# Scan operands and anchors in PSUM, the state's sum on VectorE, no idle products in the loop

## The chip, the core and the metric

The kernel runs on one core of one Trainium2 chip. The metric is the device time of one execution in microseconds. The engines run at the same time, each through its own list of instructions in order, and wait for each other by semaphores: TensorE (PE in the profile; its weight loads are PEld), VectorE (DVE), ScalarE (ACT), GpSimd (POOL) and SyncE (SP), which here only issues DMAs. SBUF is the large on-chip memory; PSUM is the small one of eight banks that TensorE writes its products to and that VectorE and ScalarE, but not GpSimd, use as well in this kernel.

## What is computed

A linear attention with decay, then a mixture of eight experts with one expert a token, then a gated feed-forward layer. The change lies in the first part and in the gate behind it:

```python
# r, k, v, w: (2, 8, 768, 48); u: (8, 48)
for t in range(768):
    cur = einsum('bhd,bhe->bhde', u * k_t, v_t)
    y[:, :, t] = einsum('bhd,bhde->bhe', r_t, state + cur)
    state = w_t[:, :, :, None] * state + einsum('bhd,bhe->bhde', k_t, v_t)
x = y as (1536, 384)
logits = x @ w_gate                    # (1536, 8); the first of the largest is the expert
disp[e, pos] = x of the tokens of e    # in order of the tokens
h = maximum(disp @ w1[e], 0); out = gate weight * (h @ w2[e])
out = (silu(out @ w_gate2) * (out @ w_val)) @ w_out
```

## The kernel before

**Chunks.** The 1536 tokens are cut into twelve chunks `u` of 128 (`C`), six for each batch (`UPB`); a chunk is two halves of 64 (`HC`). The heads lie as four pairs (`NP`), two heads of 48 in the 128 partitions. Within a chunk the recurrence is written as products: VectorE makes running products of the decays, `scores(u)` makes a masked matrix of scores, `values(u)` multiplies it with the values and adds what the state of the earlier chunks gives, and `state(u)` makes the next state.

**VectorE's preparation of a chunk.** `prep1(u)`: two scans X (L369), one for each half, over 264 columns: a running product of the decays, begun anew at each head pair by a constant second operand, `xinit`, in SBUF. `anchored(u)`: a reciprocal (L377) of every eighth column of X, written to every eighth column of `anch[u % 2]`, which is zero elsewhere. `prep2(u)`: two scans R (L415) over 256 columns, which multiply with the decays `wm` (copied by ScalarE in `prep0`) and add the anchors; then two products M (L421, L424) of k and r with X and R, which `scores(u)` and the later products read; then `prep3`, the product rk (L434).

**The other VectorE work of the loop.** `xrow(u)`: x (L533), the output y from PSUM plus the chunk's own term aV (GpSimd, L449). In `state(u)`: d (L516), the decay over the chunk's border, and the new state Sc (L519), which is the PSUM tile psP times d. `expand(u)` (ScalarE) puts the state into the tile Sb for `values(u+1)`. Small steps of the gate's choice are put between these by `tick()` when a group of four chunks is complete.

**TensorE's order in iteration u** (u = 0 to 9): `state(u)`: for chunks with an earlier state first a product of the identity with Sc (L509), which begins the sum in psP, then sixteen small products (L513); `warm`: products of constants into a bank that nobody reads (L458), three an iteration from u = 2 on; `scores(u+1)` (L469), whose results ScalarE copies out (L471) and GpSimd masks with two selects (L472); transposes of k (L480); products for the own term and the gate's logits (L441, L559) and transposes of x (L547) in `gate_t(u-1)`; `values(u)` (L494, L499); `columns` (L576), the last product for the logits. VectorE prepares chunk u+2 in iteration u, so TensorE's scores of chunk u+1 need the M that VectorE made in the iteration before. No state is made for chunks 5 and 11. `check(u)` lets ScalarE read X and anch (L386) to add up a measure of range. GpSimd has two selects and one aV an iteration, later also the scatters.

The order on every engine is that of the program; the schedule is written by hand, and the framework adds the semaphores. For PSUM it keeps any two accesses of different engines to the same bank of one tile in the order of the program, two reads included. The loop is

```python
    for u in range(NU - 2):
        if u:
            prep0(u + 2); prep1(u + 2)
        xrow(u - 1); state(u); anchored(u + 2)
        warm((7, 4)[u] if u < 2 else 3, ps1, "xT")
        scores(u + 1)
        if u: own(u)
        kgtok(u + 1); gate_t(u - 1, ...)
        expand(u); load_dm(u + 4); zero(NZ)
        ...                                  # count and place a complete group
        prep2(u + 2); check(u + 2)
        values(u); columns(u - 1, ...)
```

and chunk 10 and 11 are finished by a written-out tail (L948 on), with one state (chunk 10) and VectorE's own aV. Behind it come the experts (L1297, L1315) and the feed-forward layer (L1418, L1441).

Of the kernel before, what the change touches and what calls it, by code (L numbers as in the profile page):

```python
# [24 lines left out]
C = 128  # L25
# [4 lines left out]
G = 8  # L30
# [12 lines left out]
def build(tc, cap, dm, tk, vt, ub, cst, wg, w1, w2, wgate, wval, wout, out):  # L43
# [239 lines left out]
    ac = at.enter_context(tc.tile_pool(name="ac", bufs=1))  # L283
    xinit = ac.tile([128, 2, NP, XW], F32, name="xinit")
    csb = ac.tile([128, 3 * E], F32, name="csb")
# [4 lines left out]
    tri = ac.tile([128, 128], BF16, name="tri")  # L290
    ones = ac.tile([128, 128], BF16, name="ones")
    slots = ac.tile([128, NU], I32, name="slots")
# [7 lines left out]
    dmt = [ep.tile([128, DMW], F32, name=f"dm{i}", bufs=1) for i in range(3)]  # L300
    anch = [ep.tile([128, 2 * (NP * HC + G - 1)], F32, name=f"anch{i}", bufs=1) for i in range(2)]
    wm = [ep.tile([128, 2, NP, HC], F32, name=f"wm{i}", bufs=1) for i in range(2)]
# [4 lines left out]
    ps1 = at.enter_context(tc.tile_pool(name="ps1", bufs=1, space=PSUM))  # L307
    psY = at.enter_context(tc.tile_pool(name="psY", bufs=2, space=PSUM))

    vts, Xf, Xt, Mt, kgt, Sc, At, yt, xt, xgt, xgs, av, rkt, a8s, lgt = ({} for _ in range(15))  # L310
# [5 lines left out]

    def anchors(x, h, o):

        return x[:, h, :, h * o:h * o + HC - G + 1:G]

# [39 lines left out]
    def prep1(u):  # L360


        if u >= NU:
            return
        W = dmt[u % 3][:, 0:2 * NP * XW].rearrange("p (h a j) -> p h a j", h=2, a=NP)
        Xf[u] = ap3.tile([128, 2 * (NP * XW + G + 1)], F32, tag="X", name="X")
        X = Xt[u] = halved(Xf[u], XW)
        for h in range(2):
            nc.vector.tensor_tensor_scan(out=run(X[:, h], h), data0=run(W[:, h], h), data1=run(xinit[:, h], h),  # L369
                                         initial=0.0, op0=ALU.mult, op1=ALU.max)  # L370
            tick()

    def anchored(u):

        if u >= NU:
            return
        nc.vector.reciprocal(out=each8(anch[u % 2], HC), in_=each8(Xf[u], XW))  # L377
        tick()

    def check(u):  # L380

        if u >= NU:
            return
        for i, t in enumerate((each8(Xf[u], XW), each8(anch[u % 2], HC))):
            j = gp.tile([128, 2, NP, HC // G], F32, tag="sum", name="sum")
            nc.scalar.activation(out=j, in_=t, func=AF.Copy, accum_out=total[:, 2 * u + i:2 * u + i + 1])  # L386
# [22 lines left out]
    def prep2(u):  # L409
# [4 lines left out]
        for h in range(2):  # L414
            nc.vector.tensor_tensor_scan(out=run(Rt[:, h], 1 - h), data0=run(wm[u % 2][:, h], 1 - h),  # L415
                                         data1=run(halved(anch[u % 2], HC)[:, h], 1 - h),
                                         initial=0.0, op0=ALU.mult, op1=ALU.add)
            tick()
# [34 lines left out]
    def warm(n, ps=None, tag="T"):  # L453

        ps = (ps or psA).tile([128, 512], F32, tag=tag if ps else "A0", name="psW")
        x = xinit.rearrange("p h a j -> p (h a j)").bitcast(BF16)[:, 0:512]
        for _ in range(n):
            nc.tensor.matmul(ps, ones, x, start=True, stop=True)  # L458

# [24 lines left out]
    def values(u, ps=range(NP)):  # L484

        if not ps[0]:
            yt[u] = psY.tile([128, DM], F32, tag="y", name="y")
        y, A = yt[u], At[u]
        V = vts[u]
# [12 lines left out]
    def state(u):  # L502

        if not (u + 1) % UPB:
            return
        P = ps1.tile([128, NP, D], F32, tag="P", name="psP")
        k = kgt.pop(u)
        if u % UPB:
            nc.tensor.matmul(P, ident, Sc[u], start=True, stop=False, skip_group_check=True)  # L509
        for p in range(NP):  # L510
            for g in range(2):
                c0 = D * (2 * p + g)
                nc.tensor.matmul(P[64 * g:64 * g + 64, p, :], k[:, p, 64 * g:64 * g + 64], vts[u][:, c0:c0 + D],  # L513
                                 start=not u % UPB, stop=True, skip_group_check=True)
        d = ap2.tile([128, NP], F32, tag="d", name="d")
        nc.vector.tensor_tensor(out=d, in0=Xt[u][:, 1, :, XW - 1], in1=Xt[u + 1][:, 0, :, 0], op=ALU.mult)  # L516
        tick()
        s = Sc[u + 1] = ap2.tile([128, NP, D], F32, tag="Sc", name="Sc")
        nc.vector.tensor_tensor(out=s, in0=P, in1=d.unsqueeze(2).to_broadcast([128, NP, D]), op=ALU.mult)  # L519
        tick()  # L520
# [8 lines left out]
    def xrow(u):  # L529
        if u < 0:  # L530
            return
        x = xt[u] = gp.tile([128, DM], F32, tag="x", name="x", bufs=7)
        nc.vector.tensor_tensor(out=x, in0=yt.pop(u), in1=av.pop(u), op=ALU.add)  # L533
        tick()
# [27 lines left out]
    def logits_to(u):  # L562
        g = group[u]
        if g not in lgt:
            lgt[g] = ps1.tile([128, len(g), 3 * E], F32, tag="P" if g[-1] == NU - 3 else "lg", name="lg")
        return lgt[g][:, u - g[0]]
# [6 lines left out]
    def columns(u, w, q):  # L573

        to = logits_to(w)
        nc.tensor.matmul(to[:, 0:2 * E], gss.pop(u), fold[:, 0:2 * E], start=True, stop=True)  # L576
        a8s[q] = gp.tile([128, H], F32, tag="a8", name="a8")
        nc.scalar.copy(out=a8s[q], in_=to[:, E:2 * E])
# [22 lines left out]
    def choose(us, weigh=weigh):  # L601

        n = len(us)
        u0, u1 = us[0], us[-1] + 1
        lg = lgt[us][:, :, 0:E]

# [40 lines left out]
    def count(us):  # L647

        u0, n = us[0] // 4 * 4, len(us)
        pc = lgt[us][:, :, 2 * E:]  # L650
        adds = [(ohacc, us[0])] * (u0 > 0) + [(ohs[:, q, :], max(us[0], q + 1)) for q in range(u0, us[-1])]
# [204 lines left out]
    nc.vector.memset(xinit, TINY)  # L856
    nc.vector.memset(xinit[:, 0, :, HC:HC + 1], 1.0)
    nc.vector.memset(xinit[:, 1, :, 1:2], 1.0)
    for i in range(2):
        nc.gpsimd.memset(wm[i], 0.0)  # L860
        nc.vector.memset(anch[i], 0.0)
    nc.vector.memset(ones, 1.0)
    prep0(0)
# [16 lines left out]
    anchored(1)  # L880
    prep2(1)
    prep0(2)
    prep1(2)
    for i in range(2):
# [3 lines left out]
    for u in range(NU - 2):  # L888
        chosen, counted = ended.get(u - 2), ended.get(u - 3)
        if u:  # L890
            prep0(u + 2)
            prep1(u + 2)
        xrow(u - 1)
        state(u)
        anchored(u + 2)
        warm((7, 4)[u] if u < 2 else 3, ps1, "xT")
        scores(u + 1)
# [5 lines left out]
        else:  # L903
# [5 lines left out]
            gss.update((q, gs[:, C * q:C * q + C]) for q in range(2))  # L909
            warm(2, ps1, "lg")  # L910
        expand(u)
# [7 lines left out]
        if not u:  # L919
            check(1)  # L920
            nc.vector.tensor_copy(out=tri, in_=before)
        check(u + 2)
        if u:
            values(u)
            columns(u - 1, max(u - 2, 0), u + 1)
        else:
            values(u)
            for q in range(2):
                to = logits_to(q)
                nc.tensor.matmul(to[:, 0:E], gss.pop(q), fold[:, E:2 * E], start=True, stop=True)  # L930
            a8 = gp.tile([128, 2, H], F32, tag="a82", name="a82")
            nc.scalar.copy(out=a8, in_=lgt[group[0]][:, 0:2, 0:E])
            for q in range(2):
# [27 lines left out]
    for f in c4:  # L961
        f()
    state(u)
    values(u, [0])
    warm(1, ps1, "xT")
# [595 lines left out]
```

## Time and profile before

| | us |
|---|---|
| median of 3 runs (465.39 to 465.67) | 465.55 |
| the profiled execution | 465.57 |
| its span, first to last instruction | 463.9 |
| TensorE busy in the span | 450.2 (97%) |
| VectorE busy | 331.0 (71%) |
| ScalarE busy | 238.8 (51%) |
| GpSimd busy | 70.9 (15%) |

The busy shares are means over stages with different bounds: TensorE's 97% over the span doesn't say what bounds the attention loop, which lies between about 14 and 79 us. A stage is read from its own windows and its own timeline. In a timeline the first number is the start, the second what the instruction took to its last write, and the next independent instruction of VectorE may start some 0.1 us before that end; "x2" is two like instructions in a row, taken together. What stands in brackets behind a row is the idle time before it and what ended it. The spans on GpSimd are rough, and a few records of matmuls are missing (two of three products at 32.36, for one).

### The profile page before, as it was taken

What the parts mean: (1) busy time and instruction counts of PE and PEld (TensorE: products, weight loads), DVE (VectorE), ACT (ScalarE), POOL (GpSimd) and SP (SyncE); (2) the same over time, 40 slices, a digit from 0 to 9 for tenths busy, and PEclk for the clock granted to TensorE, in tenths of its full rate; (3) what the DMA queues carried; (4) which work ended last, traced back from release to release, by engine and by line L of the source; (5) the groups of instructions that cost most, each with busy time, mean ns of one, the idle gap of its engine ahead of it and who ended that gap; (6) DMA issues with size and microseconds to landing.
All of it is one profiled execution on the core that took longest, in us unless ns stands there. A gap on an engine that the chain in (4) does not pass through costs nothing.

```text
span 463.9 us, 9305 instructions
## 1 busy us (share of the span) xinstructions
PE 450.2 (97%) x3565; PEld 397.8 (86%) x3576; DVE 331.0 (71%) x690; ACT 238.8 (51%) x561; POOL 70.9 (15%) x94
## 2 busy tenths in 40 slices
PE   7998999999999999999999999999999999999994
PEld 3676767889999999999988888888888888888884
DVE  8999999877887945858599876665678585434241
ACT  4556685666877866674446454544443352231120
POOL 3324355540000000000000650000000000003033
PEclk9999999999999999999999999999999999999999
DMA  7798994139999944336134455222200000001011
GB/s 247 219 290 266 314 279 163 70 103 305 378 350 361 357 171 144 91 116 199 42 101 131 75 68 70 68 68 69 68 1 0 3 0 0 1 0 69 0 70 68
DMA packets 34801, 62.57 MB, mean 135 GB/s; under 512 B 5504, under 2 KB 17280, under 8 KB 34752
## 3 DMA queue, kind: packets, MB, share of 16 engines
q1 hardware_dynamic: 32832, 57.20, 40.5%
q0 software_dynamic: 1920, 4.73, 2.8%
q8 instruction: 29, 0.48, 0.5%
q14 instruction: 20, 0.16, 0.1%
HBM read 52.48 MB, written 9.44 MB: 133 GB/s over the span
## 4 chain that ended last, share of the span: by engine, by line
PE 80%; DVE 9%; issue 4%; DMA 4%; ACT 1%; POOL 1%; POOLq 0%; SPq 0%; DVEq 0%; ACTq 0%
PE psg L1418 32%; PE psu L1441 14%; PE psh L1297 14%; PE pso L1315 13%; DMA dm<-in_dm 2%; DVE R L415 2%; DVE X L369 2%; DVE M L424 1%; POOL out L1453 1%; PE psA L469 1%; PE y L494 1%; PE y L499 1%; PE psx L1282 1%; DVE rk L434 1%; DVE anch L377 1%
## 5 line engine op out<-in xcount | busy, mean ns | idle before, releaser
L1418 PE MATMUL psg<-yb,wu 128*128 128x512 f32 x648 | 156.3, 395 | 0.0
L1418 PEld LDWEIGHTS psg<-yb,wu 128*128 128x128 f32 x648 | 121.3, 188 | 26.2
L1441 PE MATMUL psu<-wu,a 128*128 128x384 f32 x432 | 80.8, 336 | 0.0
L1441 PEld LDWEIGHTS psu<-wu,a 128*128 128x128 f32 x432 | 76.4, 188 | 2.9
L1297 PE MATMUL psh<-xe,wu 128*128 128x240 f32 x576 | 69.1, 277 | 0.9 <-DVE xe L835 0.9
L1297 PEld LDWEIGHTS psh<-xe,wu 128*128 128x128 f32 x576 | 66.2, 190 | 1.2 <-DVE xe L835 1.1
L1315 PE MATMUL pso<-h,wu 128*128 128x240 f32 x576 | 66.4, 275 | 0.0
L1315 PEld LDWEIGHTS pso<-h,wu 128*128 128x128 f32 x576 | 65.4, 189 | 0.0
L1425 DVE TENSOR_TENSOR t<-t,psg 128x512 f32<-128x512 f32 x36 | 24.7, 686 | 51.9 <-PE psg L1418 38.9
L213 DVE TENSOR_TENSOR wu<-raw,wu 128x512 fp32r<-128x512 f32 x96 | 61.6, 684 | 0.0
L207 ACT CAST wu<-raw 128x512 fp32r<-128x512 f32 x96 | 54.9, 620 | 3.0 <-PE pso L1315 1.4
L1430 ACT CAST a<-t 128x512 fp32r<-128x512 f32 x36 | 22.3, 620 | 60.3 <-DVE t L1425 60.3
L1304 DVE SCALAR_TENSOR_TENSOR h<-psh,h 128x240 fp32r<-128x240 f32 x64 | 25.0, 403 | 23.2 <-ACT h L1303 22.9
L207 ACT CAST wu<-bits 128x384 fp32r<-128x384 f32 x36 | 18.0, 513 | 42.0 <-DVE bits L200 41.9
L1453 POOL DMA_INDIRECT out<-acc,idc x12 | 11.7, 975 | 173.6 <-DVE acc L1451 172.1
L1330 POOL DMA_INDIRECT idl<-ids,dests x12 | 13.5, 1124 | 159.0 <-DVE dests L795 155.6
L1424 ACT ACTIVATE t<-psg 128x512 f32<-128x512 f32 x36 | 21.5, 597 | 30.2 <-PE psg L1418 30.1
L1431 DVE TENSOR_TENSOR a<-t,a 128x512 fp32r<-128x512 f32 x36 | 24.8, 689 | 13.2 <-ACT a L1430 13.2
L1303 ACT ACTIVATE h<-psh 128x240 fp32r<-128x240 f32 x64 | 23.3, 374 | 9.8 <-PE psh L1297 9.1
L1451 DVE TENSOR_TENSOR acc<-psu,acc 128x384 f32<-128x384 f32 x24 | 12.9, 558 | 19.9 <-PE psu L1441 19.9
L471 ACT COPY A<-psA 128x512 f32<-128x512 f32 x24 | 12.8, 586 | 19.0 <-PE psA L469 19.0
L472 POOL TENSOR_SCALAR_AFFINE_SELECT A<-A 128x512 f32<-128x512 f32 x24 | 15.4, 665 | 43.6 <-ACT A L471 43.6
(156 smaller groups left out, 554.5 us busy)
## 6 DMA issues: line engine op xcount, KB each, us to landing
raw<-in_moe_w SPq DMA_DIRECT2D x32, 768.0 KB, 10.8
scr<-zrow SPq DMA_DIRECT2D x12, 384.0 KB, 4.9
raw<-in_moe_w_gate SPq DMA_DIRECT2D x6, 768.0 KB, 4.8
raw<-in_moe_w_val SPq DMA_DIRECT2D x6, 768.0 KB, 4.4
raw<-in_moe_w_out SPq DMA_DIRECT2D x6, 768.0 KB, 4.3
dm<-in_dm SPq DMA_DIRECT2D x18, 192.0 KB, 4.4
v<-in_tk SPq DMA_DIRECT2D x12, 192.0 KB, 6.5
dm<-in_dm SPq DMA_DIRECT2D x18, 99.0 KB, 4.7
```

The costliest lines, as they stand in the source:

```text
L207: nc.scalar.copy(out=slot_t[u % NSLOT][:, 0, c:c + n], in_=bits[i])
L213: nc.vector.tensor_tensor(out=w[:, 1, c:c + n], in0=bits.pop(i), in1=R(w[:, 0, c:c + n]), op=ALU.subtract)
L1297: nc.tensor.matmul(ps, w[:, a, k, c0:c0 + 128], xet[e][:, b, k, :], start=n == 0, stop=n == 8)
L1303: nc.scalar.activation(out=h[:, 0, :], in_=ps, func=AF.Relu)
L1304: nc.vector.scalar_tensor_tensor(out=h[:, 1, :], in0=ps, scalar=0.0, in1=R(h[:, 0, :]), op0=ALU.max, op1=ALU.subtract)
L1315: nc.tensor.matmul(ypt[e, d], w[:, a, f % 4, 128 * d:128 * d + 128], h[:, b, :], start=f == 0 and n == 0, stop=f == 7 and n == 2)
L1418: nc.tensor.matmul(gps[i][g], w[:, a, g, k, c0:c0 + 128], yb[t, k][:, c], start=a_ == k == 0, stop=a_ == k == 2)
L1424: nc.scalar.activation(out=t, in_=pg[0], func=AF.Silu)
L1425: nc.vector.tensor_tensor(out=t, in0=t, in1=pg[1], op=ALU.mult)
L1430: nc.scalar.copy(out=a[:, 0], in_=t)
L1431: nc.vector.tensor_tensor(out=a[:, 1], in0=t, in1=R(a[:, 0]), op=ALU.subtract)
L1441: nc.tensor.matmul(out_ps[t, j], att[i][:, c, 128 * j:128 * j + 128], w[:, a, f % 4, :], start=f % FP == 0 and n == 0, stop=f % FP == FP - ...
```

## The change

Four things change. The anchors lie in one PSUM tile, `anch`, in place of two in SBUF, and X's constant operand (now one for both halves) in PSUM beside the state's products, in the tile `tots`. The state's products are no longer added to an identity product: a new function `moved` adds the old state on VectorE, from PSUM and SBUF, then multiplies with d. `warm` in the loop stays for u = 0 and 1 alone. And as these take PSUM banks, the logits go to the end of y's bank and from there, by ScalarE's copy, to `lgs` in SBUF; the counts of the groups go to a bank of y or to anch's. `state(u)` is called ahead of `prep1(u+2)`, and `check(1)` and `state(0)` ahead of the loop.

```diff
-    xinit = ac.tile([128, 2, NP, XW], F32, name="xinit")
...
-    ones = ac.tile([128, 128], BF16, name="ones")
+    idle = ac.tile([128, 4 * C], BF16, name="idle")
+    ones = idle[:, 0:C]
...
-    anch = [ep.tile([128, 2 * (NP * HC + G - 1)], F32, name=f"anch{i}", bufs=1) for i in range(2)]
...
+    anch = ps1.tile([128, 2 * NP * HC], F32, tag="lg", name="anch")
+    tots = ps1.tile([128, NP * D + NP * XW], F32, tag="P", name="tots")
+    xinit = tots[:, NP * D:]
+    inv = anch.rearrange("p (h a j g) -> p h a j g", h=2, a=NP, g=G)[..., 0]
+    lgs = ac.tile([128, NU - 3, 2 * E], F32, name="lgs")
...
-            nc.vector.tensor_tensor_scan(out=run(X[:, h], h), data0=run(W[:, h], h), data1=run(xinit[:, h], h),
+            nc.vector.tensor_tensor_scan(out=run(X[:, h], h), data0=run(W[:, h], h), data1=xinit,
...
-        nc.vector.reciprocal(out=each8(anch[u % 2], HC), in_=each8(Xf[u], XW))
+        nc.vector.reciprocal(out=inv, in_=each8(Xf[u], XW))
...
-                                         data1=run(halved(anch[u % 2], HC)[:, h], 1 - h),
+                                         data1=turned(anch[:, h * (NP * HC - G + 1):][:, 0:NP * HC], 1 - h),
...
-            yt[u] = psY.tile([128, DM], F32, tag="y", name="y")
+            yt[u] = psY.tile([128, 512], F32, tag="y", name="y")
...
-        P = ps1.tile([128, NP, D], F32, tag="P", name="psP")
+        P = psp[u] = tots[:, 0:NP * D].rearrange("p (a d) -> p a d", a=NP)
         k = kgt.pop(u)
-        if u % UPB:
-            nc.tensor.matmul(P, ident, Sc[u], start=True, stop=False, skip_group_check=True)
...
+    def moved(u):
+
+        if u not in psp:
+            return
+        P = psp.pop(u)
         d = ap2.tile([128, NP], F32, tag="d", name="d")
         nc.vector.tensor_tensor(out=d, in0=Xt[u][:, 1, :, XW - 1], in1=Xt[u + 1][:, 0, :, 0], op=ALU.mult)
         tick()
         s = Sc[u + 1] = ap2.tile([128, NP, D], F32, tag="Sc", name="Sc")
+        if u % UPB:
+            nc.vector.tensor_tensor(out=s, in0=P, in1=Sc[u], op=ALU.add)
+            P = s
         nc.vector.tensor_tensor(out=s, in0=P, in1=d.unsqueeze(2).to_broadcast([128, NP, D]), op=ALU.mult)
         tick()
...
         g = group[u]
+        if g[-1] < NU - 4:
+            return yt[max(yt)][:, DM:DM + 2 * E]
...
+        if w < NU - 4:
+            w = w if q == w + 3 else NU - 4
+            nc.scalar.copy(out=lgs[:, w, :], in_=to)
+            a8s[q] = lgs[:, w, E:]
+            return
...
+        if us[-1] < NU - 4:
+            lgt[us] = (psY if us[-1] < NU - 5 else ps1).tile([128, n, 3 * E], F32, tag="y" if us[-1] < NU - 5 else "lg", name="lg")
...
     prep2(1)
+    check(1)
     prep0(2)
+    state(0)
     prep1(2)
...
             prep0(u + 2)
+            state(u)
             prep1(u + 2)
         xrow(u - 1)
-        state(u)
+        moved(u)
         anchored(u + 2)
-        warm((7, 4)[u] if u < 2 else 3, ps1, "xT")
+        if u < 2:
+            warm((7, 4)[u], ps1, "xT")
         scores(u + 1)
```

In the tail `moved(10)` follows `state(10)`.

## Rows read from the trace of the kernel before

**Rows 1.** The page's first line

```profile
span 463.9 us, 9305 instructions
```

**Rows 2.** Windows: busy us of PE, PEld, DVE, ACT, POOL; granted clock; DMA, GB/s

```profile
30.00:35.00 5.00, 4.95 (x84) 3.83 (x84) 4.90 (x10) 2.65 (x11) 0.48 (x1) 1.00 0.83 279
94.00:97.00 3.00, 2.17 (x16) 1.72 (x14) 2.77 (x6) 2.00 (x6) 1.30 (x2) 1.00 0.05 15
```

**Rows 3.** Timeline of VectorE, iteration 2: start, us, line, operation, out<-in

```profile
26.86 1.29 DVE L369 TENSOR_TENSOR_SCAN X<-dm,xinit 128x264 f32<-128x264 f32 x2
28.08 0.53 DVE L533 TENSOR_TENSOR x<-y,aV 128x384 f32<-128x384 f32 x1
28.53 0.58 DVE L516 TENSOR_TENSOR d<-X 128x4 f32<-128x4 f32 x1
29.21 0.36 DVE L519 TENSOR_TENSOR Sc<-psP,d 128x192 f32<-128x192 f32 x1
29.49 0.55 DVE L377 RECIPROCAL anch<-X 128x64 f32<-128x64 f32 x1
30.14 1.47 DVE L415 TENSOR_TENSOR_SCAN R<-wm,anch 128x256 f32<-128x256 f32 x2
32.11 0.68 DVE L424 TENSOR_TENSOR M<-dm,R 128x512 f32<-128x512 f32 x1
32.72 0.68 DVE L434 TENSOR_TENSOR rk<-dm 128x512 f32<-128x512 f32 x1
33.32 1.29 DVE L369 TENSOR_TENSOR_SCAN X<-dm,xinit 128x264 f32<-128x264 f32 x2
```

**Rows 4.** Timeline of TensorE from the identity product of iteration 3 to its scores

```profile
31.25 0.57 PE L509 MATMUL psP<-Sc,ident 128*128 128x192 f32 x2
32.36 0.82 PE L458 MATMUL psW<-xinit,ones 128*128 128x512 bf16 x2
33.11 1.16 PE L469 MATMUL psA<-M 64*128 64x128 f32 x16
```

**Rows 5.** Timeline of all engines, iteration 5, which has no state product

```profile
45.02 0.68 DVE L424 TENSOR_TENSOR M<-dm,R 128x512 f32<-128x512 f32 x1
45.75 1.16 PE L469 MATMUL psA<-M 64*128 64x128 f32 x16 [0.96 <-DVE M L424]
47.66 1.22 POOL L472 TENSOR_SCALAR_AFFINE_SELECT A<-A 128x512 f32<-128x512 f32 x2 [3.70 <-ACT A L471]
47.88 0.54 DVE L377 RECIPROCAL anch<-X 128x64 f32<-128x64 f32 x1
```

**Rows 6.** Timeline of VectorE, other places: undisturbed, beside a select, beside aV

```profile
5.76 1.27 DVE L415 TENSOR_TENSOR_SCAN R<-wm,anch 128x256 f32<-128x256 f32 x2
22.12 0.15 DVE L516 TENSOR_TENSOR d<-X 128x4 f32<-128x4 f32 x1
23.29 1.86 DVE L415 TENSOR_TENSOR_SCAN R<-wm,anch 128x256 f32<-128x256 f32 x2
```

**Rows 7.** Timeline of GpSimd beside these

```profile
23.33 1.28 POOL L449 TENSOR_TENSOR aV<-v,a 128x384 f32<-128x384 f32 x1
28.46 1.22 POOL L472 TENSOR_SCALAR_AFFINE_SELECT A<-A 128x512 f32<-128x512 f32 x2 [3.85 <-ACT A L471]
29.65 0.83 POOL L449 TENSOR_TENSOR aV<-v,a 128x384 f32<-128x384 f32 x1
```

**Rows 8.** Groups of VectorE instructions before 125 us: count, busy us, mean ns

```profile
L415 DVE TENSOR_TENSOR_SCAN R<-wm,anch 128x256 f32<-128x256 f32 x24 | 20.7, 899 | 1.0
L516 DVE TENSOR_TENSOR d<-X 128x4 f32<-128x4 f32 x10 | 2.3, 230 | 0.0
```

**Rows 9.** Timeline of the tail, VectorE and TensorE

```profile
82.92 0.53 DVE L533 TENSOR_TENSOR x<-y,aV 128x384 f32<-128x384 f32 x1
83.75 0.55 PE L547 MATMUL psx<-ident,x 128*128 128x128 f32 x3
```

**Rows 10.** Timeline of TensorE, the first products of the kernel

```profile
3.04 5.30 PE L458 MATMUL psW<-xinit,ones 128*128 128x512 bf16 x12 [3.04 <-DVE ones L862]
```

More of the change, by code (lines that the diff above doesn't have):

```diff
@@ L315, in run, with turned @@
         return x if up else x[:, ::-1]
-    def anchors(x, h, o):
-        return x[:, h, :, h * o:h * o + HC - G + 1:G]
+    def turned(x, up):
+        return x if up else x[:, ::-1]
     def halved(x, w):
@@ L383, in check @@
             return
-        for i, t in enumerate((each8(Xf[u], XW), each8(anch[u % 2], HC))):
+        for i, t in enumerate((each8(Xf[u], XW), inv)):
             j = gp.tile([128, 2, NP, HC // G], F32, tag="sum", name="sum")
@@ L455, in warm @@
         ps = (ps or psA).tile([128, 512], F32, tag=tag if ps else "A0", name="psW")
-        x = xinit.rearrange("p h a j -> p (h a j)").bitcast(BF16)[:, 0:512]
         for _ in range(n):
-            nc.tensor.matmul(ps, ones, x, start=True, stop=True)
+            nc.tensor.matmul(ps, ones, idle, start=True, stop=True)
     def scores(u):
@@ L486, in values @@
         if not ps[0]:
-            yt[u] = psY.tile([128, DM], F32, tag="y", name="y")
-        y, A = yt[u], At[u]
+            yt[u] = psY.tile([128, 512], F32, tag="y", name="y")
+        y, A = yt[u][:, 0:DM], At[u]
         V = vts[u]
@@ L513, in state @@
                 nc.tensor.matmul(P[64 * g:64 * g + 64, p, :], k[:, p, 64 * g:64 * g + 64], vts[u][:, c0:c0 + D],
-                                 start=not u % UPB, stop=True, skip_group_check=True)
+                                 start=True, stop=True, skip_group_check=True)
+    psp = {}
+    def moved(u):
+        if u not in psp:
+            return
+        P = psp.pop(u)
         d = ap2.tile([128, NP], F32, tag="d", name="d")
@@ L532, in xrow @@
         x = xt[u] = gp.tile([128, DM], F32, tag="x", name="x", bufs=7)
-        nc.vector.tensor_tensor(out=x, in0=yt.pop(u), in1=av.pop(u), op=ALU.add)
+        nc.vector.tensor_tensor(out=x, in0=yt.pop(u)[:, 0:DM], in1=av.pop(u), op=ALU.add)
         tick()
@@ L604, in choose @@
         u0, u1 = us[0], us[-1] + 1
-        lg = lgt[us][:, :, 0:E]
+        lg = lgs[:, u0:u1, 0:E] if u1 <= NU - 4 else lgt[us][:, :, 0:E]
         def over(x):
@@ L856, in build @@
     nc.vector.memset(xinit, TINY)
-    nc.vector.memset(xinit[:, 0, :, HC:HC + 1], 1.0)
-    nc.vector.memset(xinit[:, 1, :, 1:2], 1.0)
+    nc.vector.memset(xinit.rearrange("p (a j) -> p a j", a=NP)[:, :, 1:2], 1.0)
     for i in range(2):
         nc.gpsimd.memset(wm[i], 0.0)
-        nc.vector.memset(anch[i], 0.0)
-    nc.vector.memset(ones, 1.0)
+    nc.vector.memset(anch, 0.0)
+    nc.vector.memset(idle, 1.0)
     prep0(0)
@@ L909, in build @@
             gss.update((q, gs[:, C * q:C * q + C]) for q in range(2))
-            warm(2, ps1, "lg")
+            warm(2, psY, "y")
         expand(u)
@@ L919, in build @@
         if not u:
-            check(1)
             nc.vector.tensor_copy(out=tri, in_=before)
         check(u + 2)
+        values(u)
         if u:
-            values(u)
             columns(u - 1, max(u - 2, 0), u + 1)
         else:
-            values(u)
+            to = yt[0][:, DM:DM + 2 * E].rearrange("p (q e) -> p q e", q=2)
             for q in range(2):
-                to = logits_to(q)
-                nc.tensor.matmul(to[:, 0:E], gss.pop(q), fold[:, E:2 * E], start=True, stop=True)
+                nc.tensor.matmul(to[:, q], gss.pop(q), fold[:, E:2 * E], start=True, stop=True)
             a8 = gp.tile([128, 2, H], F32, tag="a82", name="a82")
-            nc.scalar.copy(out=a8, in_=lgt[group[0]][:, 0:2, 0:E])
+            nc.scalar.copy(out=a8, in_=to)
             for q in range(2):
@@ L963, in build @@
     state(u)
+    moved(u)
     values(u, [0])
```

## The prediction

> **What bounds the kernel now.** I read the page first: a span of 463.9 us [rows 1] in a profiled execution of 465.57 us, so 1.67 us lie around the span; the median of the runs is 465.55 us. In the chain of work that ended last, everything from the expert layers on lies on TensorE and on lines that the change leaves alone, so what the first part of the kernel gains or loses is passed on whole to the end. The diff touches the attention loop (about 14 to 79 us) and the code just before and behind it. The sums by windows come next [rows 2]: in a stretch of the loop VectorE is busy 4.90 of 5 us and TensorE 4.95, so two engines look like the bound. The timeline tells them apart. VectorE runs one iteration's ten steps with no wait for another engine, only the 0.1 us between an instruction and one that needs its result [rows 3]; 26.86 to 33.32 is 6.46 us. TensorE's 6.5 us hold 0.75 us of idle products (32.36 to 33.11) and 0.5 us of identity product (31.25, recorded 0.57) [rows 4]. Where TensorE has no state product to make, it stands 0.96 us waiting for M of L424, and starts 0.05 us after M's end at 45.70 [rows 5]. So VectorE sets the pace and TensorE, with its fillers, only just fits in. TensorE's savings alone are worth nearly nothing; the time goes as VectorE goes.
>
> **What VectorE loses to GpSimd.** The same instruction takes two lengths. Two R scans that nothing disturbs take 1.27 us; the pair at 23.29 takes 1.86, while GpSimd's product aV, 0.83 us elsewhere, takes 1.28 [rows 6, 7]. The pair at 30.14 starts inside an aV that ends at 30.48, and takes 1.47: it moves 0.14 us before that end. The tiny d at 28.53 takes 0.58, to the end of the first of two selects (28.46, 0.61 each); the d at 22.12, just as a select begins, takes 0.15 [rows 3, 6, 7]. All these VectorE instructions read two tensors in SBUF. Sc at 29.21 (one operand from PSUM) and the reciprocal at 29.49 (one operand) run through the second select and aV at their usual 0.36 and 0.55 [rows 3, 7]. So a VectorE instruction with two SBUF tensors and a GpSimd instruction that reads SBUF exclude each other, and an operand from PSUM escapes this. d came between two selects without lengthening the pair, so VectorE gets its turn there.
>
> **The change, part by part.**
> Anchors in PSUM: R reads wm from SBUF and anch from PSUM, and is no longer held. The 12 pairs hold VectorE 20.7 us [rows 8]; undisturbed they would take 12 x 1.27 = 15.2. Gain 5.5 us.
> X's constant in PSUM: every X pair of the loop already takes 1.29 us, undisturbed [rows 3]; gain nothing.
> Price of a PSUM operand on a scan: no row has one. Between SBUF tensors d takes 0.15 us for 4 elements and M 0.68 for 512 [rows 3, 6], 1.04 ns an element; by that x (384) would take 0.55 and Sc (192) 0.35, and with an operand from PSUM they take 0.53 and 0.36 [rows 3]. So it costs between -0.02 and +0.02 us; I take 0, as the two lie on either side, and 48 scans x 0.02 = 0.9 either way for the range. [...]
> Reciprocal into PSUM: no VectorE row writes there. It lies on the path 12 times; below by nothing, above by about the 0.1 us between its end and R's start [rows 3], 1.2 us in all. I take 0, as its 64 elements take 0.55 us whatever the target.
> One anch in place of two: the reciprocal of u+2 must wait for ScalarE's check of u+1. That small read now follows R, which ends at 31.6; the next reciprocal comes a period behind 29.49, at 35.95 [rows 3], 4.3 us later. Behind the check ScalarE has queued the gate copy and the two wm copies, needed an iteration later. Cost 0.
> State and X in one bank: X of u+2 must follow the state products of u, and the next state products must follow X. The products end where the idle ones begin, at 32.36, and X starts at 33.32 [rows 3, 4]; without the identity product they end earlier still. Cost 0, and 1 us of room. The state's move ahead of prep1 changes no VectorE order, since d and the product stay behind x.
> Add of the old state: d's user no longer stands 0.25 behind it; d steps on in some 0.11 (nothing and its 0.15 are the bounds), the add takes Sc's 0.36 and the 0.10 until the product that needs it, the product steps on in 0.28 as Sc did: 0.85 in place of 0.25 + 0.28 [rows 3, 6]. Cost 0.32 in each of seven loop iterations (1 to 4, 7 to 9), 2.2 us. The add itself has an operand in PSUM and isn't held.
> Where the holding goes: TensorE will start its scores 0.05 us behind M each time. By the iteration that already does so, the first select then starts 1.96 us behind M's end, and the step behind x 2.18 behind it [rows 5]. So d falls into the first select (1.96 to 2.57) and moves at about 2.43 in place of 2.18: +0.25 in five iterations (2, 3, 4, 8, 9), +1.25; before, d lost 0.8 in all (2.3 us less 10 x 0.15) [rows 8]. Net +0.45. The new product has two SBUF tensors and comes at about 3.0, just where the second select lets go: +0.04 each, +0.25 in all. aV (3.1 to 4.0) then meets the reciprocal and R, which it can't hold, and is over before M at 5.1.
> TensorE: 1.25 us less an iteration. In iteration 5 to 6 it is even again for a moment (5.45 against VectorE's 5.3), then idle for about 1 us in each. What the idle products cover, a granted clock that falls, is a rival below.
> ScalarE's gate copy takes both halves of the logits (16 columns for 8), checks of chunk 1 move ahead of the loop, counts go to other banks, memsets are shorter but end before the first load lands: nothing on the path.
> Tail: TensorE's scores start 0.3 us behind M now (32.79 to 33.11) [rows 3, 4], the last ones too, and 0.05 behind it then: -0.2. In the tail the add, and VectorE's own aV held by a select that now meets it, put x at 82.92 some 0.7 us further behind M; TensorE's transpose at 83.75 stands 0.3 behind that x [rows 9]: +0.5.
> Sum: -5.5 + 2.2 + 0.45 + 0.25 - 0.2 + 0.5 = **-2.3 us**, 465.57 to 463.27; on the median 463.2 us.
>
> **Rivals.**
> (a) More: d slips ahead of the select after all, as at 22.12 [rows 6], and the tail hides the add. Then -2.3 - 1.25 - 0.5 = -4.0, 461.5 us. For it: several iterations of now go so. Against: there TensorE was behind.
> (b) PSUM dearer: by the upper bounds, +0.9 for scans and up to 1.2 for reciprocals, against -2.3: up to 465.4, about 464.9. [...] Against: the rows of x and Sc.
> (c) Slower by the clock: the idle products go and TensorE's granted clock falls to the lower of its two levels. The first twelve products stand at 0.44 us each, those of the loop at 0.25 [rows 4, 10]; 5.2 us of work an iteration would become 9.1, over VectorE's 6.4 by 2.7, in eight iterations +21 us: about 485. It decides from a pace 6.4/5.2 = 1.2 times slower. Against: with TensorE busy 2.17 of 3 us at 94 us the granted clock is still 1.00 [rows 2]; the loop would be at 5.2 of 6.4.
> (d) The new product loses its turn to aV and waits for its 0.83 us: seven times, +5.8, 469.0. Against: d between the selects.
> (e) It doesn't do what it says: R is held all the same, since wm and the output are in SBUF. Then 2.2 + 0.45 + 0.25 + 0.3 = +3.2, about 468.7. Against: Sc under the select.
>
> **How the numbers follow.** My forecast 0.52, (a) 0.14, (b) 0.17, (c) 0.05, (d) 0.07, (e) 0.05. The likeliest gives 463.2 us. The range goes from (a), with 0.2 for faster scans, to the upper end of (b), with 0.5 for the holding of d and the product: 461.3 to 465.9. It leaves out (c), (d) and (e), 0.17. About 0.2% (0.93 us) is what a measurement of this kernel can tell from no change: faster is under 464.6, slower over 466.5. Faster: 0.48 of the forecast, (a), 0.05 of (b): 0.67. Same: 0.04 and 0.12: 0.16. Slower: (c), (d), (e): 0.17.
>
> **What would show it.** R pairs of 1.2 to 1.3 us throughout, with aV at 0.83 inside them; twelve of them about 15.2 us. The new add at 0.36 and the product at about 0.36; d at 0.3 to 0.4 behind selects. Iterations of about 6.4 us with state, 5.3 without, and TensorE waiting for M in nearly all. R or X pairs over 1.35 us away from GpSimd's instructions mean (b); scores of 1.16 us grown towards 2 mean (c); products of 1 us (d). I am wrong if the R pairs stay long, or if another engine than VectorE sets the pace.

## The result and the profile after

The changed kernel takes **468.40 us** (median of 20 runs, 465.55 to 471.64), the kernel before 465.56 beside it (20 runs, 465.39 to 465.81): 2.8 us slower, ratio 1.006 [1.0043, 1.0077]. The forecast was 463.2. The runs of the kernel before lie within 0.4 us, those of the changed one within 6, at a mean granted clock of 0.980 to 0.997 (before: 0.999). The profiled execution of the changed kernel took 466.87 us, with this first line of its page:

```profile
span 465.1 us, 9232 instructions
```

VectorE's timeline, iteration 3 (columns as in [rows 3], which it answers):

```profile
32.28 1.29 DVE L372 TENSOR_TENSOR_SCAN X<-dm,tots 128x264 f32<-128x264 f32 x2
33.49 0.53 DVE L544 TENSOR_TENSOR x<-y,aV 128x384 f32<-128x384 f32 x1
33.94 0.49 DVE L524 TENSOR_TENSOR d<-X 128x4 f32<-128x4 f32 x1
34.35 0.34 DVE L528 TENSOR_TENSOR Sc<-tots,Sc 128x192 f32<-128x192 f32 x1
34.73 0.48 DVE L530 TENSOR_TENSOR Sc<-Sc,d 128x192 f32<-128x192 f32 x1
35.14 0.55 DVE L380 RECIPROCAL anch<-X 128x64 f32<-128x64 f32 x1
35.79 1.26 DVE L418 TENSOR_TENSOR_SCAN R<-wm,anch 128x256 f32<-128x256 f32 x2
38.76 1.29 DVE L372 TENSOR_TENSOR_SCAN X<-dm,tots 128x264 f32<-128x264 f32 x2
```

R is at 1.26 us, as forecast, but from X to X it is 6.48 us, no less than the 6.46 of before. VectorE's groups before 125 us (count, busy us, mean ns), beside [rows 8]:

```profile
L418 DVE TENSOR_TENSOR_SCAN R<-wm,anch 128x256 f32<-128x256 f32 x24 | 15.2, 673 | 1.0
L530 DVE TENSOR_TENSOR Sc<-Sc,d 128x192 f32<-128x192 f32 x8 | 3.8, 480 | 0.3
L524 DVE TENSOR_TENSOR d<-X 128x4 f32<-128x4 f32 x10 | 3.2, 320 | 0.0
L528 DVE TENSOR_TENSOR Sc<-tots,Sc 128x192 f32<-128x192 f32 x8 | 2.8, 344 | 0.0
```

The R scans went from 20.7 to 15.2 us, to the tenth what the sum said; the add, d and the product take it back inside an iteration. The gain that is left lies where no add is made (the first iterations and those behind chunk 5): X of chunk 11 starts at 71.72 (before 72.99).

TensorE waits longer now. Its timeline in iteration 5, beside [rows 5], and the window from 45 us (busy us of PE, PEld, DVE, ACT, POOL; granted clock; DMA, GB/s):

```profile
44.86 1.16 PE L471 MATMUL psA<-M 64*128 64x128 f32 x16 [1.71 <-DVE M L427]
45.95 0.89 PE L482 MATMUL psT<-ident,M 128*128 128x128 f32 x4
45.00:50.00 5.00, 5.00 (x63) 3.79 (x65) 4.90 (x10) 2.66 (x8) 2.02 (x3) 0.66 1.03 321
```

The idle 0.96 us of before are 1.71, and behind them the granted clock is at the lower of the two levels that this profile shows (0.50 in place of 1.00) from 46.2 to 49.6; the transposes at 45.95 take 0.89 us for 0.66. X of chunk 8 then waits 1.3 us for state products.

The larger loss is in the tail. GpSimd's fourth scatter, SyncE's read of the scattered rows that must follow its landing, and TensorE's first product of these rows, in the kernel before and in the changed one:

```profile
89.20 0.97 POOL L750 DMA_INDIRECT scr<-xg,slots  x1 [0.30 <-ACT xg L591]
91.79 0.81 SPq L803 DMA_DIRECT2D zrow<-scr  x2
94.23 0.89 PE L829 MATMUL x<-ident,zrow 128*128 128x128 f32 x4
88.32 0.97 POOL L770 DMA_INDIRECT scr<-xg,slots  x1 [0.30 <-ACT xg L609]
93.01 0.81 SPq L823 DMA_DIRECT2D zrow<-scr  x2
95.47 0.95 PE L849 MATMUL x<-ident,zrow 128*128 128x128 f32 x4 [2.19 <-SPq L1259]
```

In the kernel before the scatter is issued at 89.20 and the read at 91.79: 2.6 us. In the changed one the scatter is 0.9 us earlier and the read 1.2 later: 4.7 us, and TensorE stands idle 2.19. The DMA view from 88 to 93 us (busy tenths and GB/s in 40 slices, then packets by queue) shows why:

```profile
DMA  0000699961000019877100000000020001000000
GB/s 0 0 0 0 258 332 369 344 246 25 0 0 0 0 74 573 332 283 295 50 0 0 0 0 0 0 0 0 0 37 0 0 0 37 0 25 0 0 0 0
q0 software_dynamic: 128, 0.39, 21.9%
q8 instruction: 1, 0.02, 2.2%
```

q0 carries the last two scatters, and the one packet of q8 is 16 KB of instructions, which I take for TensorE's, as products on TensorE alone move it (pad28, below). By the packet records it begins at 89.90 and ends at 91.67, 1.76 us later. A record doesn't name the DMA engine of its packet, but the fourth scatter moves as sixteen like chains of packets, as many as the profile counts DMA engines: fifteen are done by 90.55, and the sixteenth begins at 91.65, just as the 16 KB end. Its three packets of data start at 91.65, 92.13 and 92.40, the lone slices on the right. So I take it that this chain stood behind the 16 KB on their engine. In the kernel before the 16 KB came at 87.6, before this scatter's packets. By its records (a few are missing), TensorE has 2,572 instructions ahead of the experts, where it had 2,626. So it comes to the place at which the next 16 KB are fetched later, while the loop ends earlier, and the scatter meets the fetch.

### The profile page after: what moved, and what is told of

It reads as the page before. It is cut to its first block, busy times and chain, and to the rows that moved or that the text cites. A ratio compares the mean times of both kernels' runs of the same rounds, so it can differ in the third digit from the quotient of the medians.

```text
span 465.1 us, 9232 instructions
## 1 busy us (share of the span) xinstructions
PE 443.7 (95%) x3536; PEld 395.5 (85%) x3536; DVE 329.2 (71%) x696; ACT 238.0 (51%) x561; POOL 67.4 (14%) x94
## 4 chain that ended last, share of the span: by engine, by line
PE 74%; issue 2%; POOL 1%; DVE 1%; ACT 1%; POOLq 0%
PE psg L1440 32%; PE psu L1463 14%; PE psh L1319 14%; PE pso L1337 13%; POOL out L1475 1%; PE psx L1304 1%; DVE acc L1473 0%; PE x L849 0%; ACT wu L207 0%; POOLq L1579 0%; DVE xe L1308 0%; ACT xe L1307 0%; DVE xe L855 0%; ACT xe L854 0%; POOLq L1475 0%
## 5 line engine op out<-in xcount | busy, mean ns | idle before, releaser
L471 PE MATMUL psA<-M 64*128 64x128 f32 x192 | 14.1, 286 | 7.9 <-DVE M L427 6.7
```

## The experiments

**Theory A:** the loop's gain is as forecast; it is lost to the fetch in the scatter's way and to clock falls in TensorE's longer idle time. **Rival B:** the VectorE work of the change is the loss. **Rival C:** the clock alone, and the fetch doesn't matter.

**First set.** Idle products back; 28 tiny products ahead of the first load, which are to move the fetch and leave the loop as it is; idle products with the operands in SBUF; idle products with the identity product in place of the add.

```diff
# fill3 (idle products back)
-        if u < 2:
-            warm((7, 4)[u], ps1, "xT")
+        warm((7, 4)[u] if u < 2 else 3, ps1, "xT")
# pad28 (the changed kernel, and)
+    tiny = ps1.tile([128, 512], F32, tag="T", name="tiny")
+    for _ in range(28):
+        nc.tensor.matmul(tiny[0:16, 0:8], one8.bitcast(BF16), one8.bitcast(BF16)[:, 0:8], start=True, stop=True)
# fill3_sbuf (fill3, and)
-    anch = ps1.tile([128, 2 * NP * HC], F32, tag="lg", name="anch")
+    anch = ep.tile([128, 2 * NP * HC], F32, name="anch", bufs=1)
-    xinit = tots[:, NP * D:]
+    xinit = ep.tile([128, NP * XW], F32, name="xinit", bufs=1)
# fill3_ident (fill3, and)
+        if u % UPB:
+            nc.tensor.matmul(P, ident, Sc[u], start=True, stop=False, skip_group_check=True)
...
-        if u % UPB:
-            nc.vector.tensor_tensor(out=s, in0=P, in1=Sc[u], op=ALU.add)
-            P = s
```

Expected of fill3:

> The changed kernel with the three idle products put back into each iteration of the loop (24 in all); anchors, X's constant and the VectorE add stay as changed. Theory A (the loss is the clock's falls in the loop's idle time, plus TensorE's instruction fetch, which 56 fewer instructions moved from before the fourth scatter's issue into its transfer): the granted clock stays at 0.999 in every run, the fetch comes before the fourth scatter as in the kernel before, experts start at about 95 us and not 98, and the time is 465.6 - 2.3 = about 463.3 us, with runs within 0.3 us of each other. Rival B (the VectorE work of the change is the loss, the clock is a by-product): 466 us or more. Rival C (only the clock, and the late scatter has another cause than the instruction count): clock 0.999, zrow still late by 2 us, about 465.4 us.

Of pad28:

> The changed kernel with 28 tiny TensorE products (16x8 outputs) ahead of the first load's landing, where TensorE stands idle; nothing is added to the loop. They only move the places in TensorE's program at which code is fetched, by 56 instructions. Theory A: the clock's falls stay (mean clock of runs spread over 0.980 to 0.997, times spread over several us), but the fetch is out of the fourth scatter's way: every run is some 2.1 us faster at the same clock than the changed kernel, so 466.9 - 2.1 = 464.8 us at a clock of 0.994 and a median of about 466.3. Rival C (the scatter is late for another reason): no change, 468.4 median, 466.9 at 0.994.

Of fill3_sbuf:

> As fill3 (idle products back), but anchors and X's constant lie in SBUF, in one copy each; the state's sum stays on VectorE. It tells the worth of the PSUM operands alone. By the prediction's sum the R scans are held by GpSimd again: 24 of them 20 us or more and not 15.2, so 4 to 5.5 us slower than fill3, about 468. If PSUM operands cost as much as they save: the same as fill3.

Of fill3_ident:

> As fill3 (idle products back), but the old state is added by an identity product on TensorE as before, and VectorE has no add; anchors and X's constant stay in PSUM. By the prediction's sum VectorE saves 0.32 us in each of seven iterations and the tail's add, but TensorE then has its full 6.4 us an iteration again and may set the pace: between fill3 - 2.2 (VectorE sets the pace) and fill3 + 0.5 (TensorE does). I expect the middle, about 462.5 us if fill3 is 463.3.

Measured, beside 469.36 us for the kernel before (467.92 to 470.58) on this chip: fill3 468.29 (ratio 0.9977 [0.9966, 0.9988]), pad28 469.54 (1.000 [0.9983, 1.0017]), fill3_sbuf 469.57 (1.0002 [0.9989, 1.0015]), fill3_ident 466.74 (0.9944 [0.9926, 0.9963]). The kernel before itself takes 3.8 us more here than in the first comparison, so the changed kernel had to stand beside it before pad28 could be read. Among the four: the identity product in place of the add gains 1.55 us, and PSUM operands only 1.3, where 4 to 5.5 was expected: with its operands in SBUF, R takes 17.9 us in fill3_sbuf and not 20 or more, beside 15.2 in fill3. No fall of the clock lies in the loop in the profiles of the kernels with idle products, but fill3's runs have a mean clock of 0.991 to 0.995, where 0.999 was expected; in its profile it falls at 89.6.

**Second set.** The changed kernel and the kernel before as they are, pad28 and fill3 again.

> The changed kernel as it is, beside the kernel before on one chip. In the runs with idle products the kernel before itself took 469.4 us (465.6 on the chip of the first comparison), and TensorE's semaphores reached VectorE up to 2.4 us late while scatters were under way; so the changed kernel has to be measured beside them. Theory A (clock falls in the loop's idle time and the instruction fetch in the fourth scatter's way): on a chip where the kernel before takes 465.6, 467 to 470 us with a clock of 0.98 to 0.997; on one where it takes 469.4, 470 to 472, that is 1 to 2 us over the kernel with 28 tiny products ahead. Rival C (the fetch doesn't matter): the same as that kernel within 0.5 us.

> The kernel before, for a profile on the same chip as the others. Where it takes 465.6 us: clock 0.999, no wait of VectorE for a late semaphore. Where it takes 469.4: VectorE waits 1 to 2.5 us about 88 to 91 us for a product of TensorE that had long ended, as in the four runs so far, TensorE stands idle 2 us behind it, and the clock falls once there; then this loss is the chip's and not the change's.

> The changed kernel with 28 tiny products ahead of the first load, once more, now beside the changed kernel itself. Theory A: 1 to 2.1 us faster than the changed kernel, the fetch at 88 us in place of 90, the read of the scattered rows issued 2.6 us behind the last scatter and not 4.7. Rival C: the same within 0.5 us.

> The changed kernel with the idle products back, beside the changed kernel and the kernel before on one chip. Theory A: no fall of the clock before 85 us; 463.3 us where the kernel before takes 465.6 (-2.3, the predicted gain); where that takes 469.4, 468.3 as in the first run, and 1 to 3 us under the changed kernel. Rival B (the VectorE work is the loss): no faster than the changed kernel.

Measured, beside 469.31 for the kernel before: the changed kernel 470.5 (ratio 1.0009 [0.9993, 1.0025]), pad28 468.63 (0.9994 [0.9978, 1.0011]), fill3 468.33 (0.9981 [0.9968, 0.9994]). The profile of the kernel before on this chip, VectorE's step, TensorE's next product, and two windows:

```profile
90.92 0.17 DVE L709 TENSOR_TENSOR t<-lg,ohs 128x16 f32<-128x16 f32 x1 [1.97 <-PE lg L571]
92.51 0.17 PE L652 MATMUL lg<-ohs,tri 128*128 128x16 bf16 x1 [2.01 <-DVE ohs L630]
93.00:96.00 3.00, 3.00 (x8) 2.56 (x9) 2.86 (x14) 2.33 (x5) 1.15 (x4) 0.50 0.31 114
96.00:99.00 3.00, 3.00 (x12) 2.69 (x12) 2.14 (x6) 1.41 (x4) 2.59 (x5) 0.55 0.18 68
```

The brackets name L571 as what t waits for, but in the first comparison's profile t starts at 88.27, just behind the counts (L655) and ahead of L571's end. Here L655 (88.56 for 0.17 us) had ended by 88.8 and L571 by 89.4, yet t starts at 90.92; TensorE idles 2.0 us for what follows, and the clock is at its lower level from within that time on. In all eight profiles of these two sets, of the kernel before and of changed ones, TensorE idles 2.0 to 2.4 us at this place, so it is no effect of the change; its cause stays open. It also takes away what pad28 was to test: with TensorE 2.3 us late, the changed kernel's fetch falls behind the scatter by itself (read issued 2.6 us behind it), so the 1.9 us between the changed kernel and pad28 here can't be put down to the fetch. Their runs overlap (468.40 to 471.61 and 467.37 to 470.14), and what makes this difference stays open.

**Third set.** Idle products in two iterations; the identity product back without idle products; the kernel before without idle products; fill3_ident again.

```diff
# fill57 (the changed kernel, and)
-        if u < 2:
-            warm((7, 4)[u], ps1, "xT")
+        warm((7, 4)[u] if u < 2 else 3 if u in (5, 7) else 0, ps1, "xT")
# ident0: the two edits of fill3_ident to the changed kernel, without those of fill3
# bnofill (the kernel before, and)
-        warm((7, 4)[u] if u < 2 else 3, ps1, "xT")
+        if u < 2:
+            warm((7, 4)[u], ps1, "xT")
```

> The changed kernel with three idle products in iterations 5 and 7 only (6 in all, where the kernel with all of them back has 24). In the changed kernel's records TensorE's two longest idle stretches of the loop lie there (1.71 us at 44.86, 1.25 us at 58.42; 0.7 to 1.03 elsewhere), and each fall seen in the loop began within 2 us behind one of these. Theory A1 (the long stretches alone bring the falls): the clock holds in the loop, and the time is that of the kernel with all idle products back, 468.3 us where the kernel before takes 469.3, or less by some tenths, since TensorE has more room. Theory A2 (every idle stretch counts): falls elsewhere in the loop remain, 469 to 470.5.

> The changed kernel with the identity product back in place of VectorE's add, and without idle products. It tells whether 0.5 us of identity product an iteration hold the clock as the idle products do; iteration 5, which has no state, stays without either. Theory A: falls remain, and VectorE gains the add (1.55 us by the pair with idle products): about 470.5 - 1.5 = 469 us where the kernel before takes 469.3. If the identity product is enough: 466 to 467, as with idle products.

> The kernel before with one edit of the change alone: no idle products in the loop from its third iteration on. The working of the prediction put nothing for this. Theory A (idle TensorE brings the clock down): 0.75 us an iteration go, TensorE's wait in iteration 5 grows from 1 to 1.7 us, and the clock falls once or more in the loop in most runs: 1 to 2.5 us slower than the kernel before. Rival B (only VectorE's work counts): the same as the kernel before, or 0.3 us faster.

> PSUM operands, identity product and idle products: of the change's four parts only the anchors and X's constant in PSUM. Once more with more rounds, as it was the fastest so far: 466.7 us where the kernel before takes 469.4, ratio 0.994; where the kernel before takes 465.6, about 462.9.

This chip is like that of the first comparison: 465.65 us for the kernel before (465.45 to 465.88). fill57 465.96 (ratio 1.002 [1.0004, 1.0036]), **ident0 459.96 (0.9882 [0.9868, 0.9896])**, bnofill 465.62 (1.0001 [0.9992, 1.001]), fill3_ident 462.84 (0.9939 [0.9926, 0.9952]).

Only fill3_ident came out as expected. bnofill was to be 1 to 2.5 us slower and is the same, though TensorE idles nearly as long there as in the changed kernel:

```profile
45.52 1.16 PE L469 MATMUL psA<-M 64*128 64x128 f32 x16 [1.58 <-DVE M L424]
```

Four of its ten runs have a clock of 0.990 to 0.992 and take 465.9 to 466.1 us, the six others (0.996 to 0.998) 465.3 to 465.7: the lower mean clock goes with half a microsecond, but no such run was profiled. And ident0 was to be 0.3 us faster than the kernel before or, at best, some 3 (469 or 466 beside 469.3): it is 5.7 us faster and beats every other kernel here. Its VectorE and GpSimd in iteration 2, TensorE's scores behind M, and VectorE's group of d (the profile is of its slowest run, 462.53 us, with a fall of the clock from 54.3 to 61.1, behind this place):

```profile
26.69 0.53 DVE L543 TENSOR_TENSOR x<-y,aV 128x384 f32<-128x384 f32 x1
27.14 0.15 DVE L526 TENSOR_TENSOR d<-X 128x4 f32<-128x4 f32 x1
27.33 0.36 DVE L529 TENSOR_TENSOR Sc<-tots,d 128x192 f32<-128x192 f32 x1
28.27 1.26 DVE L418 TENSOR_TENSOR_SCAN R<-wm,anch 128x256 f32<-128x256 f32 x2
30.03 0.69 DVE L427 TENSOR_TENSOR M<-dm,R 128x512 f32<-128x512 f32 x1
27.18 1.22 POOL L474 TENSOR_SCALAR_AFFINE_SELECT A<-A 128x512 f32<-128x512 f32 x2 [3.57 <-ACT A L473]
31.08 1.16 PE L471 MATMUL psA<-M 64*128 64x128 f32 x16
L526 DVE TENSOR_TENSOR d<-X 128x4 f32<-128x4 f32 x10 | 1.5, 153 | 0.0
```

With the identity product TensorE's scores start 0.36 us behind M, the select starts just behind d, and Sc has an operand in PSUM: nothing is held, and an iteration takes 5.75 us. bnofill and ident0 differ in the PSUM operands (and in what made room for them, the state products' earlier place among it): 5.7 us.

fill57 was to be 1.0 us faster than the kernel before and is 0.3 slower. It has no fall in its profile's loop, and its marks run 2.0 to 2.4 us ahead of the kernel before up to the fourth scatter. Then its fetch meets the scatter as in the changed kernel (88.89, 1.83 us; read issued 4.8 us behind the scatter), and the clock falls 1.3 us after TensorE's wait for the rows, from 95.9 to 102.7:

```profile
94.59 1.02 PE L849 MATMUL x<-ident,zrow 128*128 128x128 f32 x4 [2.42 <-SPq L1258]
96.00:99.00 3.00, 2.11 (x10) 1.84 (x10) 1.22 (x3) 0.72 (x3) 2.53 (x5) 0.50 0.29 99
```

Seven of its twelve runs (clock 0.997 to 0.999) take 465.2 to 466.0 us, the other five (0.990 to 0.994) 467.4 to 468.8.

**Fourth set,** to settle the fetch and the add: pad28 again; fill57 with 22 tiny products (with their weight loads 44 instructions, beside the 12 of its idle products); and that kernel with d ahead of x.

```diff
# dfirst (fill57_pad22, and)
+        border(u)          # makes d
         xrow(u - 1)
-        moved(u)           # d, add, product
+        moved(u)           # add, product
```

> The changed kernel with 28 tiny TensorE products ahead of the first load, nothing else. Where the kernel before takes 465.6 us, the changed kernel took 468.4. Theory A (the fetch in the scatter's way stops TensorE 2.2 us): the fetch comes ahead of the scatter, no wait of TensorE at the identity products of the placing, and the falls of the clock in the loop stay: 466.2 us, with some runs at 463.5 to 464.5. Rival (the fetch is harmless): 468.4.

> Idle products in iterations 5 and 7, and 22 tiny products ahead of the first load (12 + 44 instructions, as many as the change took away). With the idle products alone the kernel took 466.0 us where the kernel before takes 465.65; its profile has the last select's marks 2.0 to 2.4 us ahead of the kernel before up to the fourth scatter, then a wait of 2.4 us for the rows behind it. Theory A: without that wait 463.4 us, no run over 464.5. Rival: 466.

> As the kernel with idle products in two iterations and 22 tiny products, but VectorE makes d ahead of x and not behind it. Theory A (0.33 us an iteration of the add's price is d held by the first select, which starts 1.96 us behind M's end, when d is late by some 0.1): d takes 0.15 us and not 0.47 to 0.50 in the iterations with a state, iterations of 6.15 us and not 6.48, 1.5 to 2.5 us faster, about 461.5. Rival (the hold moves on to x, the add or the product): no faster by more than 0.5.

Measured, beside 465.61 for the kernel before: **pad28 463.87 (ratio 0.9975 [0.9961, 0.9989])**, **fill57_pad22 463.73 (0.9961 [0.9948, 0.9973])**, dfirst 463.62 (0.9956 [0.9943, 0.9969]). With twenty-eight products that do nothing, ahead of its first data, the changed kernel takes 4.5 us less than in the first comparison. The two didn't run side by side, but the kernel before takes 465.56 and 465.61 us beside them; and at the same mean clock, 0.994, the changed kernel's four runs take 465.55 to 466.87 us and pad28's three 463.84 to 463.87. The same three rows of pad28's profile, its fetch at 85.2:

```profile
86.73 0.98 POOL L770 DMA_INDIRECT scr<-xg,slots  x1 [0.30 <-ACT xg L609]
89.31 0.81 SPq L823 DMA_DIRECT2D zrow<-scr  x2
91.86 0.94 PE L849 MATMUL x<-ident,zrow 128*128 128x128 f32 x4 [0.17 <-DMA zrow<-scr]
```

2.6 us from scatter to read, and a wait of 0.17 us in place of 2.19. fill57 to fill57_pad22 gives the stall without the falls: 465.9 (the middle of its seven runs at 0.997 and over) to 463.73, 2.1 us. The rest of the 4.5 us I put down to falls of the clock, behind the stall and in the loop, as the changed kernel's mean clock was mostly lower (0.980 to 0.997); that is argued, and how they divide was not separated. Something like the unexplained 1.9 us of the second set may be in it as well. In pad28, whose loop has no idle products, six runs of nine are at 463.4 to 464.2 and three, with a clock of 0.991 or 0.992, at 465.1 to 466.0. Theory A had 466.2 as the median, with the falls of the loop in most runs; so it had the fetch right and these falls too large. The profiled run, the fastest at 463.35, has a fall in the loop all the same (57.3 to 60.7).

dfirst made d short and gained nothing, as the rival said:

```profile
33.78 0.14 DVE L525 TENSOR_TENSOR d<-X 128x4 f32<-128x4 f32 x1
33.83 0.55 DVE L552 TENSOR_TENSOR x<-y,aV 128x384 f32<-128x384 f32 x1
34.30 0.34 DVE L536 TENSOR_TENSOR Sc<-tots,Sc 128x192 f32<-128x192 f32 x1
34.68 0.83 DVE L538 TENSOR_TENSOR Sc<-Sc,d 128x192 f32<-128x192 f32 x1
34.07 1.22 POOL L474 TENSOR_SCALAR_AFFINE_SELECT A<-A 128x512 f32<-128x512 f32 x2 [4.36 <-ACT A L473]
```

The add, with its operand from PSUM, runs through the select; the product, whose operands both lie in SBUF, now waits to the end of the second one, 0.83 us in place of 0.48. The hold moved from d (0.49 us in the same iteration of fill57_pad22, 0.14 here) to the product, the next instruction with two SBUF operands (0.48 there, 0.83 here).

**The steps of the change, one by one,** from three sets, in each of which the kernel before takes 465.6:

| kernel | us | step |
|---|---|---|
| before | 465.6 | |
| no idle products (bnofill) | 465.62 | 0.0 |
| and operands in PSUM (ident0) | 459.96 | -5.7 |
| and the add on VectorE, fetch out of the way (pad28) | 463.87 | +3.9 |
| the change, fetch in the scatter's way | 468.40 | +4.5 |

Rival C is out, as moving the fetch changes the time with the loop as it is. Of rival B this much holds: the add takes back 3.9 of the 5.7 us, which still leaves a gain. Of theory A the fetch's part is shown, and that of the falls is argued.

## Why the prediction was wrong

**What failed** is the account of TensorE: "TensorE: 1.25 us less an iteration" counted the removed instructions as time alone, and put nothing for the length of the program. By the table that omission is worth up to 4.5 us, of which 2.1 are shown to be the stall itself, and no rival held it. The tail's term ends at TensorE's transposes of x [rows 9]; the scatter behind them, read 2.6 us after its issue in the kernel before and 4.7 in the changed one, is not in the sum. That 468.40 lies near the figures of rivals (d) and (e) is chance, as neither's mechanism came. TensorE's instructions come by DMA as well in these traces, 16 KB at a time on q8, 29 packets in the span of either kernel; with 28 tiny products put ahead of the first data the one at the scatter went from 89.90 to 85.2 us. So I put which data transfer they meet down to the count of instructions in front. In the changed kernel the cost fell on a data transfer, and was 2.1 us without the falls.

**The sum came out near, with the fetch out of the way.** Then the changed work gives -1.9 us (fill57_pad22) and -1.7 (pad28), against the forecast of -2.3; 463.7 to 463.9 lies inside the forecast's range, 468.40 does not. These are other kernels than the forecast one, and their gain is 0.4 to 0.6 us short. Term by term:
- *R in PSUM, -5.5:* 15.2 us of R as forecast, so rival (e) is out. The time falls by 5.7 from bnofill to ident0, but that the two figures are so near is in part luck: between these kernels R gives 4.2 (19.5 to 15.3) and d, no longer held by the selects, 1.7 (3.2 to 1.5). In fill3 the same operands were worth 1.3.
- *Price of PSUM operands, 0:* X pairs take 1.29 us before and after, R 1.26 beside 1.27, the reciprocal 0.55. Rival (b) is out.
- *Add, d and product, +2.9 in all (2.2, 0.45, 0.25):* the way was right, the size too small. In fill57_pad22 the adds take 2.8 us; d, held in more iterations than the five forecast, took 3.5 us in all, where 2.3 + 0.45 was forecast; the products 0.49 each in place of 0.36 + 0.04. Against ident0 the add costs 3.8 us (463.73 to 459.96). I priced it against the kernel before, in which d loses time to the selects as well, and so missed that with the identity product, and scores 0.3 us later, neither d nor the product is held by a select once R is free (ident0's rows).
- *TensorE's savings alone, "worth nearly nothing":* 0.0 by bnofill. With R free and the identity product kept they are worth 2.9 us (fill3_ident 462.84, ident0 459.96), since TensorE's 6.5 us an iteration are then the bound (from 30 to 35 us it is busy 4.95 of 5 in fill3_ident, VectorE 4.62).
- *Tail, +0.3:* from M of chunk 11 to the fourth scatter fill57_pad22's lead on the kernel before shrinks from 2.4 to 2.0 us: 0.46, so the way was right.
- *Rival (c), the clock:* it had the mechanism and a wrong size. I priced a lasting fall at +21 us; what came were short ones, of 3.4 to 6.8 us. In the loop of kernels with the fetch out of the way they cost 0.1 us at the median (pad28 beside fill57_pad22, which differ in six idle products as well) and up to 2.3 in single runs; behind the tail's stall some 2.7 (fill57's five runs beside its seven, 468.6 and 465.9 at the middle). The first twelve products' 0.44 us, from which I took the +21, stand at a granted clock of 1.00 (3.00 to 9.00 us of the kernel before), so they don't show the lower level.
- *Rival (d), the product behind aV:* no; it was held by the second select, by 0.13 us.

## What to carry to other kernels

Undo a change part by part before judging it: here one part gained 5.7 us, one cost 3.9, one did nothing, and an effect of the program's length, which is none of these parts, cost up to 4.5 and decided the sign. Where VectorE and GpSimd work side by side, count the VectorE instructions with two SBUF operands and move one operand of the longest to PSUM (R went from 20.7 to 15.2 us here); getting a small one out of the way merely handed the hold to the next (dfirst). When instructions are added or taken out, look in the DMA records where the instruction transfers now fall, and if one meets a transfer that somebody waits for, try a few idle instructions ahead of the kernel's first data, which moved it here from 89.90 to 85.2 us.

## What the runs showed of the hardware that was not expected

- In the changed kernel's profile a 16 KB transfer of TensorE's instructions took 1.76 us, and one of a scatter's sixteen chains of packets moved only as it ended; the other fifteen were done by 90.55, this one at 92.52.
- The granted clock fell in or soon behind idle stretches of TensorE of 1.2 to 2.4 us, in some executions of a kernel and not in others of the same kernel, and came back 3.4 to 6.8 us after its fall with TensorE at work.
- On two of the chips each kernel that ran on the others as well took 2.1 to 5.7 us more, the one before 469.36 and 469.31 beside 465.6: a product of TensorE released VectorE up to 2.0 us late at about 89 us, while scatters were landing, and the clock fell behind it. What sets these chips apart stays open.
